# Layer two's gate and value of the last two blocks as one 2x2 block product with seven products

## The chip, the cores and the metric

One core of a Trainium2 chip runs the whole kernel in one launch. The metric is the device time of a run in microseconds, the median over runs; lower is better. The engines are TensorE (PE: matmuls; PEld is its weight load), VectorE (DVE), ScalarE (ACT), GpSimd (POOL) and the DMA queues, of which SyncE (SP) issues all the transfers named here. Each engine works through its own instructions in order and waits for others by semaphores.

## The reference

Attention over 2304 tokens, then two feed-forward layers of width 512. The change is in the second.

```python
attn_out = _attn_ref(**attn_kwargs)            # dense on a mean over 4, plus local
x = ...reshape(B * S, H * D)                   # 2304 x 512
h = x @ w_in                                   # layer one, 512 x 2048
g = np.maximum(h, 0.0) + alpha * np.minimum(h, 0.0)
x = g @ w_out
xn = x / rms * rms_g                           # layer two, 512 x 1536
g = xn @ w_gate
silu = g * (1.0 / (1.0 + np.exp(-g)))
val = xn @ w_val
return silu * val @ w_out
```

## The kernel before

**Numbers.** Every f32 operand of a large product is split into a high and a low f16 half, and a product is made as high x high, high x low and low x high. A product over 512 = KK x 128 inputs so takes 4 x 3 = 12 matmuls. `split` and the pairs "ACT copy to f16, DVE subtraction" make the halves.

**Stages.** The tokens are cut into six blocks (0 to 5) of BW = 384. `m1(m)` is layer one of a block: `h_mm` (L1416, tile hps; ACT relu L1420, DVE L1422), then `o_mm` (L1433, tile acc), copied out by `m1_evac` (L1447) into x1. `rms_tasks(m)` makes the norm of a block: ACT squares (L1349), sums over partitions on PE, a power on POOL (L1375), a broadcast on PE, and per 128 inputs a product (L1390) and a split.

`m2(m, slot)` is layer two of a block, in NF2 = 12 slices f of 128 hidden values. `h_part(f)` makes the gate and the value (`proj`, L1533, tile gps, 12 matmuls of 384 columns each), a tanh on ACT (L1542, th), (th + 1) x gate on DVE (L1544), times value and a scale on DVE (L1547), and the halves uhl: high on ACT (L1553), low on DVE (L1554). `o_part(f)` (L1562) multiplies three groups of 128 tokens by w_out: 9 matmuls of 512 columns into the accumulators oacc0 to oacc2, two slices behind. At the end of a block each accumulator is copied by ACT (L1618) into ob, of which there is one buffer, and stored by SP; so the next copy waits for the store. Block 5 is special: its halves are written in a permuted order (three groups, 32 by 4) so that the output rows lie together, its last two slices run accumulator by accumulator (`o_last`, L1580), and `store_last` (L1586 to L1592) copies each accumulator half on ACT and half on DVE.

**Banks.** The PSUM tags are a0 to a3 (one bank each), w (two) and at (two). The accumulators acc and oacc lie in a0 to a3, gate and value in w, w, a3 in turn.

**Order.** The program is written as a loop over stages (L1755), with side work (attention of later blocks, weight decoding, norms) put between the slices from the queues `urgent` and `bg`, as the tables `feed` and `rms_at` say. `issue_order` then sets the order of every engine by a list scheduler with modelled durations; the table LEADS shifts priorities of ranges of instructions (first, end, by how much), counted in program order. After the first blocks the stages are m2(0), m2(1), m1(2), m1(3), m2(2), m2(3), m1(4), m1(5), m2(4), m2(5).

## Time and profile before

| | us |
|---|---|
| median of 3 runs | 960.71 (960.42 to 963.69) |
| span of the profiled execution | 957.0 |
| TensorE busy in it | 928.3 |
| VectorE busy | 676.8 |
| ScalarE busy | 481.4 |
| GpSimd busy | 128.0 |

The median is 3.7 us longer than the span of the profiled execution. Layer two of block 3 ends near 680 us, m1(4) and m1(5) run to about 805, m2(4) to about 880, m2(5) to the end.

The page gives busy times, slices and groups of instructions; the windows give busy times in a chosen stretch; the chain of waits follows the last instruction back through what released each step; the timeline lists single instructions. A matmul's record lasts until its last value has drained, so the mean duration of a group is longer than the distance from one matmul to the next.

### The profile page before, as it was taken

The page shows a single profiled execution, that of the slowest core. Times are in us where ns is not written, and L with a number is a line of the kernel's source. Part 1 is how long each engine was busy: PE and PEld are TensorE (multiplying, and loading weights), DVE is VectorE, ACT ScalarE, POOL GpSimd, SP SyncE. Part 2 cuts the span into 40 slices and gives each one's busy share as a digit, 9 for nine tenths or more (in the row PEclk, how much of TensorE's full clock was granted, in tenths as well). Part 3 has the DMA queues.
Part 4 walks back from the last instruction along what each step waited for, and adds up shares of the span by engine and source line. Part 5 has one row for each costly group of instructions (what it writes and reads, how often), then busy time and mean ns, then how long its engine had stood idle before and what let it go on. Part 6 is the DMA issues. An engine that isn't in the chain of part 4 may idle for free.

```text
span 957.0 us, 16449 instructions
## 1 busy us (share of the span) xinstructions
PE 928.3 (97%) x6484; PEld 599.6 (63%) x6484; DVE 676.8 (71%) x1333; ACT 481.4 (50%) x1108; POOL 128.0 (13%) x103
## 2 busy tenths in 40 slices
PE   6978999999999999999999999999999999999998
PEld 5667877799555565556666655555566666555554
DVE  4789996899999968999977899973333342442333
ACT  5899989889872472233576322222332433221322
POOL 1101100211022003332102323220000000000000
PEclk9999999999999999999999999999999999999999
DMA  9976444574221241121032120200000000000000
GB/s 214 278 253 177 130 143 130 196 234 137 72 74 58 91 150 50 55 78 55 25 88 84 50 65 20 50 18 1 23 12 1 1 2 1 1 1 12 23 1 34
DMA packets 53711, 73.79 MB, mean 77 GB/s; under 512 B 22190, under 2 KB 35138, under 8 KB 53634
## 3 DMA queue, kind: packets, MB, share of 16 engines
q1 hardware_dynamic: 53634, 72.74, 25.3%
q8 instruction: 51, 0.84, 0.4%
q14 instruction: 26, 0.21, 0.1%
HBM read 68.01 MB, written 4.72 MB: 76 GB/s over the span
## 4 chain that ended last, share of the span: by engine, by line
PE 78%; ACT 4%; DMA 3%; DVE 3%; issue 1%; SPq 0%; ACTq 0%
PE gps L1533 26%; PE acc L1433 16%; PE hps L1416 16%; PE oacc L1562 14%; DMA out_dram<-ob 3%; PE avps L749 1%; PE sps L709 1%; PE atps L737 1%; DMA wr<-in_moe_w_gate_dram 1%; ACT wr L1165 1%; ACT w L415 1%; DVE prod L575 1%; PE xps L612 1%; DVE hps L1422 1%; DVE wc L1167 0%
## 5 line engine op out<-in xcount | busy, mean ns | idle before, releaser
L1416 PE MATMUL hps<-xt,wi 128*128 128x192 f16 (+1 forms) x1536 | 345.9, 289 | 6.6 <-DVE g L416 4.3
L1533 PE MATMUL gps<-x,w 128*128 128x384 f16 x1728 | 349.5, 326 | 0.6 <-ACT x L1447 0.4
L1433 PE MATMUL acc<-ghl,wo 128*128 128x384 f16 (+1 forms) x960 | 249.4, 310 | 0.5 <-ACT ghl L415 0.4
L1533 PEld LDWEIGHTS <-w 128*128 128x128 f16 x1728 | 169.4, 98 | 116.5 <-issue 2.6
L1562 PE MATMUL oacc<-w,uhl 128*128 128x512 f16 x630 | 200.4, 379 | 1.8 <-ACT ob L1618 1.7
L1416 PEld LDWEIGHTS <-wi 128*128 128x128 f16 x1536 | 148.0, 100 | 59.3 <-issue 7.7
L1433 PEld LDWEIGHTS <-wo 128*128 128x128 f16 x1344 | 128.8, 99 | 60.0 <-issue 2.6
L1422 DVE SCALAR_TENSOR_TENSOR hps<-g,oma,hps 128x192 f32<-128x192 f32 (+1 forms) x128 | 66.1, 517 | 66.1 <-ACT g L1420 65.4
L1542 ACT ACTIVATE th<-gps,tsc 128x384 f32<-128x384 f32 x72 | 41.7, 581 | 124.2 <-PE gps L1533 123.9
L1562 PEld LDWEIGHTS <-uhl 128*128 128x128 f16 x630 | 61.8, 98 | 64.3 <-issue 2.5
L1544 DVE SCALAR_TENSOR_TENSOR th<-th,gps 128x384 f32<-128x384 f32 x72 | 39.6, 551 | 84.9 <-ACT th L1542 84.7
L1553 ACT ACTIVATE uhl<-gps 128x384 f16<-128x384 f32 x72 | 41.7, 579 | 107.0 <-DVE gps L1547 98.5
L1420 ACT ACTIVATE g<-hps 128x384 f32<-128x384 f32 x96 | 47.0, 489 | 95.7 <-PE hps L1416 95.4
L521 POOL TENSOR_TENSOR prod<-cq,ckv 128x896 f32<-128x896 f32 x24 | 53.1, 2213 | 172.9 <-DVE ls L532 52.2
L1433 PE MATMUL acc<-g,wo 128*128 128x384 f16 (+1 forms) x384 | 69.8, 286 | 0.0
L1554 DVE TENSOR_TENSOR uhl<-gps,uhl 128x384 f16<-128x384 f32 x72 | 45.4, 630 | 28.4 <-ACT uhl L1553 28.1
L575 POOL TENSOR_TENSOR prod<-ls,ckv 128x896 f32<-128x896 f32 x24 | 47.9, 1997 | 126.4 <-issue 54.8
L416 DVE SCALAR_TENSOR_TENSOR ghl<-hps,grp,ghl 128x384 f16<-128x384 f32 (+1 forms) x73 | 44.3, 608 | 27.0 <-ACT ghl L415 26.7
L415 ACT ACTIVATE ghl<-hps,grp 128x384 f16<-128x384 f32 (+1 forms) x73 | 41.9, 574 | 40.2 <-DVE hps L1422 37.2
L532 DVE TENSOR_REDUCE ls<-prod 128x14 f32<-128x896 f32 x48 | 51.0, 1076 | 0.0
L1162 ACT ACTIVATE wr<-wr 128x768 f32<-128x768 f32 (+1 forms) x48 | 41.5, 874 | 8.7 <-DMA wr<-in_moe_w_val_dram 4.9
L1547 DVE SCALAR_TENSOR_TENSOR gps<-th,kap,gps 128x384 f32<-128x384 f32 x60 | 37.1, 618 | 9.6 <-PE gps L1533 7.0
(240 smaller groups left out, 1143.4 us busy)
## 6 DMA issues: line engine op xcount, KB each, us to landing
wr<-in_moe_w_out_dram SPq DMA_DIRECT2D x18, 512.0 KB
wr<-in_moe_w_in_dram SPq DMA_DIRECT2D x10, 768.0 KB
wr<-in_moe_w_gate_dram SPq DMA_DIRECT2D x8, 768.0 KB
wr<-in_moe_w_val_dram SPq DMA_DIRECT2D x8, 768.0 KB
ckv<-in_k_dram SPq DMA_DIRECT2D x7, 768.0 KB
ckv<-in_v_dram SPq DMA_DIRECT2D x7, 768.0 KB
wr<-in_moe_w_out_dram SPq DMA_DIRECT2D x20, 256.0 KB
sd<-in_q_dram SPq DMA_DIRECT2D x24, 144.0 KB
```

The costliest lines, as they stand in the source:

```text
L415: nc.scalar.activation(out=hi, in_=src, func=AF.Copy, scale=s)
L416: nc.vector.scalar_tensor_tensor(out=lo, in0=src, scalar=s, in1=hi, op0=ALU.mult, op1=ALU.subtract)
L521: engs[i].tensor_tensor(out=pr, in0=view(st["q"][:, j, t:t + TP], [[D, TP], [0, ND], [1, D]]), in1=view(st["k"][:, j, t:t + TP], [[D, TP], ...
L532: nc.vector.tensor_reduce(out=st["s"][:, j, t:t + TP], in_=st.pop(("p", i)), axis=AX.X, op=ALU.add)
L575: engs[i].tensor_tensor(out=over(pr, i), in0=view(st["s"][:, j, t:t + TP], [[ND, TP], [1, ND], [0, D]]), in1=view(st["v"][:, j, t:t + TP], ...
L1416: nc.tensor.matmul(ps[:, j], wi[:, f + j, a, kk * 128:(kk + 1) * 128], x[:, b_, kk, c0:c0 + n], start=(i == 0), stop=(i == 3 * KK - 1))
L1420: nc.scalar.activation(out=g, in_=ps, func=AF.Relu, scale=-1.0)
L1422: nc.vector.scalar_tensor_tensor(out=ps[:, j], in0=g[:, j], scalar=oma[:, f + j:f + j + 1], in1=ps[:, j], op0=ALU.mult, op1=ALU.add)
L1433: nc.tensor.matmul(acc[e], wo_f(f)[:, a, e * 128:(e + 1) * 128], hl[:, b_], start=(f == f0 and i == 0), stop=(f == f1 and i == 2))
L1533: nc.tensor.matmul(ps, w2_t[i0 + f // 3].rearrange("p a (k c) -> p a k c", k=KK)[:, a, kk, (f % 3) * 128:(f % 3 + 1) * 128], xh[:, b_, kk] ...
L1554: nc.vector.tensor_tensor(out=t1, in0=vp, in1=t0, op=ALU.subtract)
L1562: nc.tensor.matmul(acc[tt], t[:, a, tt * 128:(tt + 1) * 128], w[:, b_, f % 3], start=(f in first and i == 0), stop=(f in last and i == 2))
```

## The change

Layer two of blocks 4 and 5 becomes one stage, `m2_pair`. For one slice f the gate and value weights, each cut into two halves of the 512 inputs, form a 2x2 block matrix, and the two blocks of tokens, each cut in the same way, another. Their product is made by Strassen's method (in Winograd's form) with seven block products of 6 matmuls instead of eight. Three of the partial results are copied out of a bank while it still accumulates (`snap`: ACT, L1753, PSUM into SBUF), and three are added to such a copy (`plus`: DVE, L1756). Gates are then read from SBUF (tanh L1760, DVE L1761), and the halves are made by `halves` (ACT L1637, DVE L1638), permuted for block 5 alone. The second products follow for all twelve slices, in the banks a0, at, w, a1, at, a2 and with the copy in two halves; block 4's rows go out by `rows_out`, block 5's as before.

The sums and differences of weights are made by `pair_w` (per three slices 4 additions on POOL, 4 operations on DVE and 4 pairs of halves, all 768 wide), those of the inputs by `pair_x` (4 subtractions on DVE and the halves). They are kept in slices of layer one's weights whose last use is past, and in buffers that are free. In program order three of the four sets of weights are written in m2(3); the scheduler places them all, on POOL, DVE and ACT, among the slices of m1(4) and m1(5), and leaves the differences of the inputs and the norms in m2(3). The norms of blocks 4 and 5 move into layer two of block 3, local attention step 11 into m1(4), and the stages now run m2(2), m1(4), m1(5), m2(3), pair. Some scales change (P_N, P_U, P_G). The table LEADS is the same but for its line breaks, with 63 entries more at its end, whose first are shown.

```diff
-    (2930, 2948, 23500), (2582, 2585, -16500),
...
+    (5918, 6055, 3000), (2930, 2948, 23500), (2582, 2585, -16500), (6303, 6355, -2500), (6304, 6360, -1000),
+    (7303, 7478, 6000), (6691, 6718, -23500), (6590, 6615, -1000), (6906, 7280, 12500), (5813, 5946, 5500),
...
-    P_N, P_U = 10, 44
+    P_N, P_U, P_G = 8, 38, 13
...
+                if m >= PAIR:
+                    y = pair_y(m, e)
+                    nc.vector.scalar_tensor_tensor(out=y, in0=x1_t[m][:, e], scalar=rgx[:, e:e + 1], in1=st["r"],
+                                                   op0=ALU.mult, op1=ALU.mult)
+                    if m == PAIR or e >= KK // 2:
+                        halves(xh_t[m][:, 0, e], xh_t[m][:, 1, e], y)
+                    return
...
-            if m == NBLK - 1:
-                vp = vp.rearrange("p (x t c) -> p x t c", x=NT, c=NC)
-                t0, t1 = [x.rearrange("p (x c t) -> p x t c", x=NT, c=NC) for x in (t0, t1)]
...
-        def o_last():
-            for tt in range(NT):
-                for f in range(NF2 - LA, NF2):
-                    w = w2_t[8 + f // 3].rearrange("p a (f e) -> p a f e", f=3)
-                    for i, (a, b_) in enumerate(((0, 0), (0, 1), (1, 0))):
-                        nc.tensor.matmul(acc[tt], uhl[f][:, a, tt * 128:(tt + 1) * 128], w[:, b_, f % 3],
-                                         start=False, stop=(f == NF2 - 1 and i == 2))
...
+            rows_out(o, m, tt)
+
+    PAIR = NBLK - 2
+    K2 = KK // 2
+    PW = K2 * UC
...
+    def halves(hi, lo, x):
+        nc.scalar.activation(out=hi, in_=x, func=AF.Copy)
+        nc.vector.tensor_tensor(out=lo, in0=x, in1=hi, op=ALU.subtract)
+
+    def pair_y(m, e):
+        o = 6 * 2 * BW + ((m - PAIR) * KK + e) * BW
+        return wo[:, o:o + BW]
...
+        def sub(o, a, b):
+            nc.vector.tensor_tensor(out=o, in0=a, in1=b, op=ALU.subtract)
+
+        def put(n, x):
+            halves(tx[n][:, 0], tx[n][:, 1], x.rearrange("p (k n) -> p k n", k=K2))
+
+        def f1():
+            sub(b11, b12, b11)
+            put(1, b11)
+
+        def f2():
+            sub(b11, b22, b11)
+            put(2, b11)
+
+        def f3():
+            sub(b12, b22, b12)
+            put(3, b12)
+
+        def f4():
+            sub(b21, b21, b11)
+            put(4, b21)
...
+        def full(n):
+            def f():
+                w = w2_t[i + 4 * (n // 2)][:, :, (n % 2) * PW:(n % 2 + 1) * PW]
+                nc.gpsimd.tensor_tensor(out=tmp(n), in0=w[:, 0], in1=w[:, 1], op=ALU.add)
+            return f
+
+        def comb(n, o, a, b, op):
+            def f():
+                nc.vector.tensor_tensor(out=tmp(o), in0=tmp(a), in1=tmp(b), op=op)
+                d = sw[i, n] = pair_dst(i, n)
+                halves(d[:, 0], d[:, 1], tmp(o))
+            return f
+
+        return [full(0), full(2), full(3), full(1), comb(1, 3, 2, 3, ALU.add), comb(3, 2, 0, 2, ALU.subtract),
+                comb(2, 0, 3, 0, ALU.subtract), comb(4, 1, 1, 0, ALU.subtract)]
...
+    def m2_pair():
+        ma, mb = PAIR, PAIR + 1
+        NT = BW // 128
+        scr = [outd_p.tile([128, BW], F32, tag="outd", name="sn") for _ in range(2)]
+        lo = att.tile([128, 2, BW], F32, tag="lo", name="sn")
+        scr += [lo[:, 0], lo[:, 1]]
+        for i in range(4):
+            scr += [w2_t[4 + i][:, a, 0:PW].bitcast(F32) for a in range(2)]
+        last = {}
...
+        def product(ps, w, x, c, start):
+            n = 0
+            for kk in range(K2):
+                for a, b_ in ((0, 0), (0, 1), (1, 0)):
+                    nc.tensor.matmul(ps, w[:, a, kk, c:c + 128], x[:, b_, kk], start=(start and n == 0),
+                                     stop=(n == 3 * K2 - 1), skip_group_check=True)
+                    n += 1
+
+        def snap(o, ps):
+            nc.scalar.activation(out=o, in_=ps, func=AF.Copy)
+
+        def plus(o, ps):
+            nc.vector.tensor_tensor(out=o, in0=ps, in1=o, op=ALU.add)
+
+        def gate(f, g, pool, tag):
+            th = pool.tile([128, BW], F32, tag=tag, name="th")
+            nc.scalar.activation(out=th, in_=g, func=AF.Tanh, scale=tsc[:, f // 3:f // 3 + 1])
+            nc.vector.scalar_tensor_tensor(out=th, in0=th, scalar=1.0, in1=g, op0=ALU.add, op1=ALU.mult)
+            return th
+
+        def value(f, u, v, h):
+            nc.vector.scalar_tensor_tensor(out=u, in0=u, scalar=kap[:, f // 3:f // 3 + 1], in1=v, op0=ALU.mult,
+                                           op1=ALU.mult)
+            t = uhl(f)[:, h]
+            t0, t1 = t[:, 0], t[:, 1]
+            if h:
+                u = u.rearrange("p (x t c) -> p x t c", x=NT, c=NC)
+                t0, t1 = [x.rearrange("p (x c t) -> p x t c", x=NT, c=NC) for x in (t0, t1)]
+            halves(t0, t1, u)
+
+        xa, xb = xh_t[ma], xh_t[mb]
+        b11, b21, b22 = xa[:, :, 0:K2], xa[:, :, K2:KK], xb[:, :, K2:KK]
+        for f in range(NF2):
+            i, c = f // 3, f % 3 * 128
+            s = [sw[i, n].rearrange("p a (k c) -> p a k c", k=K2) for n in range(1, 5)]
+            s1_, s2_, s3_ = [scr[(3 * f + n) % len(scr)] for n in range(3)]
+            ta, tb, tf = f"a{f % 3}", "at", ("w", "w", "a3")[f % 3]
+            A = pool_of(ta).tile([128, BW], F32, tag=ta, name="pa")
+            B_ = pool_of(tb).tile([128, BW], F32, tag=tb, name="pb")
+            F_ = pool_of(tf).tile([128, BW], F32, tag=tf, name="pf")
+            product(A, wv(i, 0), b11, c, True)
+            snap(s1_, A)
+            product(B_, wv(i, K2), b21, c, True)
+            plus(s1_, B_)
+            ga = gate(f, s1_, wk, "mm")
+            product(A, s[1], tx[2], c, False)
+            snap(s2_, A)
+            product(F_, s[0], tx[1], c, True)
+            product(A, s[2], tx[3], c, False)
+            snap(s3_, A)
+            plus(s3_, F_)
+            product(F_, s[3], b22, c, False)
+            plus(s2_, F_)
+            gb = gate(f, s2_, hl_p, "hl")
+            product(A, wv(4 + i, K2), tx[4], c, False)
+            value(f, ga, A, 0)
+            value(f, gb, s3_, 1)
...
+        for h, m in enumerate((ma, mb)):
+            for tt in range(NT):
+                n = h * NT + tt
+                tag = ("a0", "at", "w", "a1", "at", "a2")[n]
+                acc = pool_of(tag).tile([128, DM], F32, tag=tag, name="oacc")
+                for f in range(NF2):
+                    w = w2_t[8 + f // 3].rearrange("p a (f e) -> p a f e", f=3)
+                    for i, (a, b_) in enumerate(((0, 0), (0, 1), (1, 0))):
+                        nc.tensor.matmul(acc, uhl(f)[:, h, a, tt * 128:(tt + 1) * 128], w[:, b_, f % 3],
+                                         start=(f == 0 and i == 0), stop=(f == NF2 - 1 and i == 2))
+                TQ = 128 // NC
+                tag = "prod" if h == 0 else "raw"
                 o = pool_of(tag).tile([128, DM], F32, tag=tag, name="ob")
-                nc.scalar.activation(out=o, in_=acc[tt], func=AF.Copy, scale=col(INV2))
-            TQ = 128 // NC
-            t_abs = m * 2 * T + tt * TQ
-            done = 0
-            while done < TQ:
-                b, t = divmod(t_abs + done, TT)
-                step = min(TQ - done, TT - t)
-                if b == 0 or b == 1 and t < T:
-                    dst = out[b * S + t * NC:b * S + (t + step) * NC, :]
+                HD = DM // 2
+                nc.scalar.activation(out=o[:, 0:HD], in_=acc[:, 0:HD], func=AF.Copy, scale=col(INV2))
+                nc.vector.tensor_scalar(out=o[:, HD:DM], in0=acc[:, HD:DM], scalar1=col(INV2), scalar2=None,
+                                        op0=ALU.mult)
+                if h:
+                    b, t = divmod(m * 2 * T + tt * TQ, TT)
+                    assert t + TQ <= TT and b > 0
+                    nc.sync.dma_start(out=bass.AP(tensor=out.tensor, offset=out.offset + (b * S + t) * DM,
+                                                  ap=[[TT * DM, NC], [DM, TQ], [1, DM]]), in_=o)
                 else:
-                    r0, TL = (CW - T, TT - T) if b == 1 else (0, TT)
-                    dst = bass.AP(tensor=out.tensor, offset=out.offset + (b * S + r0 + t) * DM,
-                                  ap=[[DM, step], [TL * DM, NC], [1, DM]])
-                nc.sync.dma_start(out=dst, in_=o[done * NC:(done + step) * NC])
-                done += step
+                    rows_out(o, m, tt)
...
-        ("m2", 3): local(11),
+        ("m1", 4): local(11),
+        ("m1", 5): pair_w(0),
     }
 
-    rms_at = {"o1": 0, ("m2", 0): 1, ("m1", 3): 2, ("m2", 2): 3, ("m1", 5): 4, ("m2", 4): 5}
+    rms_at = {"o1": 0, ("m2", 0): 1, ("m1", 3): 2, ("m2", 2): 3}
 
     def start(key):
         bg.extend(feed.get(key, []))
+        if key == ("m2", 3):
+            urgent.extend(rms_tasks(PAIR) + rms_tasks(PAIR + 1) + pair_x())
+            for i in (1, 2, 3):
+                bg.extend(pair_w(i))
...
-    for kind, m in (("m2", 0), ("m2", 1), ("m1", 2), ("m1", 3), ("m2", 2), ("m2", 3), ("m1", 4), ("m1", 5), ("m2", 4), ("m2", 5)):
+    for kind, m in (("m2", 0), ("m2", 1), ("m1", 2), ("m1", 3), ("m2", 2), ("m1", 4), ("m1", 5), ("m2", 3)):
...
+    m2_pair()
```

Three places show the new order. First ACT where block 3's (before: block 4's) accumulators are copied out and the next stage starts. Before, ob is the copy of an accumulator, th and uhl are the next block's tanh and high half:

```order
L1542 ACTIVATE th_9706<-gps_9693,tsc_121 128x384
L1553 ACTIVATE uhl_9723<-gps_9709 128x384
L1618 ACTIVATE ob_9753<-oacc0_9208,sc_105 128x512
L1542 ACTIVATE th_9779<-gps_9766,tsc_121 128x384
L1618 ACTIVATE ob_9756<-oacc1_9209,sc_105 128x512
L1553 ACTIVATE uhl_9796<-gps_9782 128x3x4x32
L1542 ACTIVATE th_9812<-gps_9799,tsc_121 128x384
L1553 ACTIVATE uhl_9829<-gps_9815 128x3x4x32
L1618 ACTIVATE ob_9760<-oacc2_9210,sc_105 128x512
L1542 ACTIVATE th_9845<-gps_9832,tsc_121 128x384
```

After, wo and xc hold the halves of the inputs' differences, and sn is the first snapshots' tile:

```order
L1637 ACTIVATE xc_8712<-wo_108 128x768
L1629 ACTIVATE ob_9309<-oacc0_8675,sc_105 128x512
L1637 ACTIVATE xc_8712<-wo_108 128x768
L1753 ACTIVATE sn_9318<-pa_9321 128x384
L1753 ACTIVATE sn_9319<-pa_9321 128x384
L1629 ACTIVATE ob_9312<-oacc1_8676,sc_105 128x512
L1760 ACTIVATE th_9338<-sn_9318,tsc_121 128x384
L1753 ACTIVATE sn_9320<-pa_9321 128x384
L1753 ACTIVATE sn_9320<-pa_9384 128x384
L1753 ACTIVATE w2_2779<-pa_9384 128x384
L1629 ACTIVATE ob_9315<-oacc2_8677,sc_105 128x512
L1760 ACTIVATE th_9401<-sn_9320,tsc_121 128x384
```

The copies ob stand among the snapshots (sn, w2), the tanhs and the last halves of the inputs, instead of among one tanh and one high half per slice.

Second, ACT inside the stage. Before, block 5 alternates:

```order
L1542 ACTIVATE th_9845<-gps_9832,tsc_121 128x384
L1553 ACTIVATE uhl_9862<-gps_9848 128x3x4x32
L1542 ACTIVATE th_9887<-gps_9874,tsc_121 128x384
L1553 ACTIVATE uhl_9904<-gps_9890 128x3x4x32
L1542 ACTIVATE th_9929<-gps_9916,tsc_121 128x384
L1553 ACTIVATE uhl_9946<-gps_9932 128x3x4x32
L1542 ACTIVATE th_9971<-gps_9958,tsc_121 128x384
```

After, in the pair (pa is the bank with the chain, sn and w2 the places of snapshots; wo holds the high halves, 128x3x4x32 the permuted ones):

```order
L1753 ACTIVATE sn_9318<-pa_9573 128x384
L1760 ACTIVATE th_9527<-w2_3685,tsc_121 128x384
L1760 ACTIVATE th_9558<-w2_4015,tsc_121 128x384
L1753 ACTIVATE sn_9319<-pa_9573 128x384
L1637 ACTIVATE wo_108<-th_9558 128x3x4x32
L1753 ACTIVATE sn_9320<-pa_9636 128x384
L1753 ACTIVATE sn_9320<-pa_9573 128x384
L1637 ACTIVATE wo_108<-th_9527 128x384
L1760 ACTIVATE th_9590<-sn_9318,tsc_121 128x384
L1753 ACTIVATE w2_2779<-pa_9636 128x384 x2
L1753 ACTIVATE w2_3320<-pa_9699 128x384
L1760 ACTIVATE th_9621<-sn_9319,tsc_121 128x384
```

Between two snapshots of one slice there now stand up to two tanhs or high halves of other slices.

Third, the start of SP's queue: loads of q, k and v (wo, sdv), of small rows, and of layer one's weights (wr). Before:

```order
L795 DMA wo_108<-in_k_dram 96x6x64
L795 DMA wo_108<-in_q_dram 96x6x64
L1143 DMA wr_663<-in_moe_w_in_dram 128x2x768
L795 DMA wo_108<-in_q_dram 96x6x64
L795 DMA wo_108<-in_k_dram 96x6x64
L803 DMA sdv_160<-in_v_dram 72x2x512
L1695 DMA rows_176<-in_moe_alpha_dram 16x128
L1695 DMA rows_176<-in_moe2_rms_g_dram 4x128
L1143 DMA wr_665<-in_moe_w_in_dram 128x2x768
```

After:

```order
L813 DMA wo_108<-in_k_dram 96x6x64
L813 DMA wo_108<-in_q_dram 96x6x64 x2
L813 DMA wo_108<-in_k_dram 96x6x64
L821 DMA sdv_160<-in_v_dram 72x2x512
L1888 DMA rows_176<-in_moe_alpha_dram 16x128
L1161 DMA wr_663<-in_moe_w_in_dram 128x2x768
L1888 DMA rows_176<-in_moe2_rms_g_dram 4x128
L813 DMA wo_108<-in_q_dram 96x6x64
L821 DMA sdv_166<-in_v_dram 72x2x512
```

The first load of layer one's weights now stands behind a load of q, k, v and the small rows that it used to precede, and the second (wr_665) further back.

## Rows read from the trace of the kernel before

**Rows 1.** Busy table of the page; then PE in 40 slices, in tenths

```profile
PE 928.3 (97%) x6484; PEld 599.6 (63%) x6484; DVE 676.8 (71%) x1333; ACT 481.4 (50%) x1108; POOL 128.0 (13%) x103
...
PE   6978999999999999999999999999999999999998
```

**Rows 2.** Windows: stretch, length, busy us of each engine, granted clock, DMA share, GB/s

```profile
0.00:128.00 128.00, 109.29 (x1003) 87.81 (x1003) 102.56 (x282) 110.19 (x320) 15.37 (x43) 0.97 0.74 209
...
240.00:260.00 20.00, 17.95 (x128) 11.79 (x128) 18.82 (x34) 16.69 (x26) 1.84 (x1) 1.00 0.19 63
...
678.00:805.00 127.00, 127.00 (x783) 76.98 (x782) 47.77 (x85) 43.67 (x86) 0.85 (x1) 1.00 0.03 7
805.00:880.00 75.00, 75.00 (x434) 42.66 (x433) 27.47 (x50) 20.31 (x42) 0.85 (x1) 1.00 0.00 1
880.00:900.00 20.00, 18.12 (x107) 10.29 (x106) 6.41 (x9) 6.09 (x9) 0.00 (x0) 1.00 0.14 39
900.00:950.00 50.00, 50.00 (x281) 27.24 (x279) 19.51 (x27) 14.11 (x18) 0.00 (x0) 1.00 0.00 1
950.00:957.00 7.00, 2.60 (x12) 0.89 (x10) 1.66 (x4) 1.42 (x3) 0.00 (x0) 0.88 0.30 112
```

**Rows 3.** Chain of waits, late part: start us, us, engine, line, instructions

```profile
809.97 5.85 PE gps L1533 x36
...
874.78 3.90 PE oacc L1562 x18
878.71 0.70 ACT ob L1618
879.42 5.84 DMA out_dram<-ob
885.34 0.70 ACT ob L1618
886.65 7.50 DMA out_dram<-ob
894.25 0.70 ACT ob L1618
894.99 0.81 PE oacc L1562 x3
```

**Rows 4.** Groups of instructions: gate and value matmuls

```profile
L1533 PE MATMUL gps<-x,w 128*128 128x384 f16 x1728 | 349.5, 326 | 0.6 <-ACT x L1447 0.4
```

**Rows 5.** Timeline of ACT after block 3: start, us, instruction, idle before

```profile
680.02 0.69 ACT L1618 ACTIVATE ob<-oacc,sc 128x512 f32<-128x512 f32 x1 [1.76 <-PE oacc L1562]
...
686.66 0.69 ACT L1618 ACTIVATE ob<-oacc,sc 128x512 f32<-128x512 f32 x1 [1.61 <-DMA out_dram<-ob]
...
693.27 0.69 ACT L1618 ACTIVATE ob<-oacc,sc 128x512 f32<-128x512 f32 x1 [1.22 <-DMA out_dram<-ob]
```

**Rows 6.** Groups by form, whole span: operations that the pair repeats

```profile
L1420 ACT ACTIVATE g<-hps 128x384 f32<-128x384 f32 x96 | 47.0, 489 | 95.7 <-PE hps L1416 95.4
...
L1542 ACT ACTIVATE th<-gps,tsc 128x384 f32<-128x384 f32 x72 | 41.7, 581 | 124.2 <-PE gps L1533 123.9
...
L1544 DVE SCALAR_TENSOR_TENSOR th<-th,gps 128x384 f32<-128x384 f32 x72 | 39.6, 551 | 84.9 <-ACT th L1542 84.7
...
L1547 DVE SCALAR_TENSOR_TENSOR gps<-th,kap,gps 128x384 f32<-128x384 f32 x60 | 37.1, 618 | 9.6 <-PE gps L1533 7.0
...
L1390 DVE TENSOR_TENSOR ra<-x,rps 128x384 f32<-128x384 f32 x24 | 12.7, 548 | 3.8 <-PE rps L1381 3.6
```

**Rows 7.** Groups by form, 900 to 957 us: the permuted halves of block 5

```profile
L1553 ACT ACTIVATE uhl<-gps 128x384 f16<-128x384 f32 x9 | 9.2, 1027 | 12.7 <-DVE gps L1547 12.7
L1554 DVE TENSOR_TENSOR uhl<-gps,uhl 128x384 f16<-128x384 f32 x9 | 9.1, 1015 | 10.4 <-ACT uhl L1553 10.4
```

**Rows 8.** Waits of PE, 0 to 130 us: total us, times, longest

```profile
PE hps L1416 <- DVE g L416: 4.3, 4, 2.5
PE tps L844 <- DMA wo<-in_q_dram: 4.1, 2, 3.0
```

More of the change, by code (lines that the diff above doesn't have):

```diff
@@ L1301, in f @@
             e, sc_ = eb2[:, i:i + 1], sw2[:, i:i + 1]
-            pow2(y, e, sc_, P_W, over_parts(y))
+            pow2(y, e, sc_, P_G if i < 8 else P_W, over_parts(y))
             if i < 4:
                 nc.vector.tensor_scalar(out=tsc[:, i:i + 1], in0=e, scalar1=rg2[:, 1:2],
-                                        scalar2=0.5 * 2.0 ** -(P_N + P_W), op0=ALU.mult, op1=ALU.mult)
+                                        scalar2=0.5 * 2.0 ** -(P_N + P_G), op0=ALU.mult, op1=ALU.mult)
             elif i >= 8:
@@ L1518, in m1_first, with rows_out @@
                         acc = m1_acc(n)
+    def rows_out(o, m, tt):
+        TQ = 128 // NC
+        t_abs = m * 2 * T + tt * TQ
+        done = 0
+        while done < TQ:
+            b, t = divmod(t_abs + done, TT)
+            step = min(TQ - done, TT - t)
+            if b == 0 or b == 1 and t < T:
+                dst = out[b * S + t * NC:b * S + (t + step) * NC, :]
+            else:
+                r0, TL = (CW - T, TT - T) if b == 1 else (0, TT)
+                dst = bass.AP(tensor=out.tensor, offset=out.offset + (b * S + r0 + t) * DM,
+                              ap=[[DM, step], [TL * DM, NC], [1, DM]])
+            nc.sync.dma_start(out=dst, in_=o[done * NC:(done + step) * NC])
+            done += step
     def m2(m, slot):
@@ L1602, in m2 @@
                 h_part(f)
-            if f >= LA and not (ends and f >= NF2):
+            if f >= LA:
                 o_part(f - LA)
@@ L1606, in m2 @@
                 slot(f, NF2)
-        if ends:
-            o_last()
         for tt in range(NT):
@@ new lines, with pair_dst @@
+    sw = {}
+    stmp = {}
+    def pair_dst(i, n):
+        u = 4 * i + n - 1
+        if u < 4:
+            if ("r", u // 2) not in sw:
+                sw["r", u // 2] = raw_p.tile([128, 2 * PW], F32, tag="raw", name="wsr")
+            return sw["r", u // 2][:, u % 2 * PW:(u % 2 + 1) * PW].bitcast(F16).rearrange("p (a w) -> p a w", a=2)
+        if u < 14:
+            o = (u - 4) * 2 * PW
+            return wi.rearrange("p f a c -> p (f a c)")[:, o:o + 2 * PW].rearrange("p (a w) -> p a w", a=2)
+        if u == 14:
+            sw["x"] = x1_p.tile([128, 2 * PW], F32, tag="x1", name="wsx")
+        return sw["x"][:, (u - 14) * PW:(u - 13) * PW].bitcast(F16).rearrange("p (a w) -> p a w", a=2)
@@ new lines, in pair_w, with tmp @@
+    def pair_w(i):
+        st = {}
+        def tmp(n):
+            if not stmp:
+                r = raw_p.tile([128, 2 * PW], F32, tag="raw", name="wt")
+                stmp[0], stmp[1] = r[:, 0:PW], r[:, PW:2 * PW]
+                for j in (2, 3):
+                    stmp[j] = prod_p.tile([128, PW], F32, tag="prod", name="wt")
+            return stmp[n]
+        def full(n):
[11 more added lines that the diff above has]
+                comb(2, 0, 3, 0, ALU.subtract), comb(4, 1, 1, 0, ALU.subtract)]
```

39 lines of the change are left out of this document (22 added, 17 removed), and 71 rows, old and new, of the table LEADS.

## Prediction

> **What bounds the kernel now.** I read the busy table first: TensorE (PE) is busy 97% of the span, VectorE (DVE) 71%, ScalarE (ACT) 50% [rows 1]. A matmul that goes is therefore worth nearly its full time, as long as PE does not begin to wait where it goes. The slices show where PE has gaps: almost only in the first tenth [rows 1]. The windows put numbers on that [rows 2]: of 28.7 us of idle PE (957.0 - 928.3), 18.7 lie in the first 128 us, 2.05 in 240 to 260, 1.88 in 880 to 900, 4.4 in the last 7. From 678 to 880 and from 900 to 950, layer two's last stretches among them, PE has no gap at all, at a granted clock of 1.00, the 2.4 GHz level, while DVE is busy 38 to 39% and ACT 28 to 34%. The change acts in that last part, so its price list is PE's.
>
> What a matmul costs there is not its row in the table of groups: a record of 326 ns [rows 4] includes a drain that lies beside the next one. The chain of waits gives the step: 36 matmuls of 384 columns in 5.85 us, 162.5 ns each, and 18 of 512 columns in 3.90 us, 216 ns each [rows 3]. The drain, 326 - 162.5, says instead when a result may be read: some 0.2 us after the last matmul's slot.
>
> The Trainium skill ("TensorE: Matmul & The Clock Gate", section "Back-to-back issue gap") says that in a long stream of weight load and matmul the spacing is about 81 ns at 128 columns and 131 ns at 512, and that the width divided by 2.4 plus 2.5 holds for a lone matmul only. Between its two figures 384 columns would take an estimated 114 ns, and the 72 removed matmuls would be worth 8.2 us. The rows above, taken in just such a stream, are 162.5 and 216, which is the formula that it keeps for the lone one; I go by the rows.
>
> **The products.** Gate and value of blocks 4 and 5 took 12 slices f, each 24 matmuls in each of two blocks: 576. With seven products of 6 matmuls it is 42 per f, 504 in all. The other four blocks keep theirs, and the second products (oacc) stay 216 in number. So 72 matmuls of 384 columns go: 72 x 0.1625 = **-11.7 us**, all of it in a stretch without idle time.
>
> **The bubble between blocks 4 and 5.** PE waits there because there is one output buffer: an accumulator can be copied out only when the store of the one before has landed. The chain shows it [rows 3]: copy 0.70, transfer 5.84, copy 0.70, transfer 7.50, copy 0.70, and only then oacc. With both blocks in one stage this hand-over is gone: **-1.9 us** (all idle of 880 to 900). Another takes its place, block 3 to the pair. There the copies are 6.64 us apart as at 680.02, 686.66 and 693.27 [rows 5]. In the new order the first product needs bank a0, free after the first copy; f=1 needs a1, free 6.64 + 0.69 after that copy began, and PE gets to it some 7.1 us after it, by the number of matmuls between; so it is late by about **+0.3 us**. Bank a2, for f=2, is reached another 6.8 us on, about when it comes free. On ACT the second and third copies wait in line for a store, with snapshots and tanhs behind them; I leave this in the upper bound of the next term.
>
> **What the pair needs from ACT and DVE.** Each f now has a chain through one bank: product, snapshot into SBUF, product on top, snapshot, product, snapshot, product, value. A snapshot is a copy of 384 columns from PSUM: 489 ns, as L1420 [rows 6]. Per f ACT has 3 of these, two tanhs of 581, a plain copy (priced as L1420 too) and a permuted one of 1.03 [rows 6, 7]: 4.15 us. DVE has 3 sums of 548 (as L1390, SBUF with PSUM), two of 551, two of 618, a plain remainder (priced as L1390 too) and a permuted one of 1.01 [rows 6, 7]: 5.5 us. PE has 42 x 0.1625 = 6.83 us. So PE remains the bound by load, with ACT at 61% and DVE at 80%, double what they had there [rows 2].
>
> By latency it is closer. Between two products on one bank PE's order has 5 to 7 matmuls of other products, 0.81 to 1.14 us; a snapshot needs 0.2 + 0.49 + 0.05 = 0.74. That fits if ACT is free. If a tanh stands ahead of it, it is 1.3, with the permuted copy 1.8, and PE waits up to 0.5 to 0.9 us. ACT's order puts tanhs and copies between the snapshots in every f, as the change section shows. The second chain has 10 to 15 matmuls, 1.6 to 2.4 us, for a snapshot and a sum of 1.3, and rarely waits. I walked f=4 and f=5 through all five orders with the durations above: PE waited 0.58 us in the two together, about 0.25 per f, **+3 us** in 12. Bounds: 0, if each snapshot comes just in time; +6.6, if in every f one snapshot stands behind one tanh (0.55 each).
>
> **What hides the preparation.** Sums of weights (16 on GpSimd, 16 on DVE, each then halved by ACT and DVE) stand in layer one of blocks 4 and 5, the differences of the inputs and the norms of blocks 4 and 5 in layer two of block 3. For a 768-wide sum on DVE twice L1547's 618 ns is enough: 32 x 1.24 = 40 us, beside 16 on ACT (16 x 2 x 0.49). The cover is a stretch of some 200 us in which DVE is at 38% and ACT at a third of PE's time [rows 2], and GpSimd does nearly nothing (0.85 of 127): cost **0**. Without that cover it would show as idle PE in front of the first product. Halving the differences has least room: it stands ahead of the first copy of block 3's output on ACT.
>
> **The early order.** The table of leads shifts also loads, weight decodes and matmuls of the first 130 us and around 200 to 260 us; from about the tenth gate of layer one the two orders agree again. PE waits there 4.3 us for DVE's gates and 4.1 for a load [rows 8], both among what moved. No row prices a reordering: **0**, between -2 (the gap of 240 to 260 gone) and +3 (a load late by the longest that one kept PE waiting, 3.0).
>
> **End.** The last two accumulators still end one after the other, with the same halves and the same fast stores: 0.
>
> **Rivals.**
> (a) The orders fit better than my walk: no waits in the pair, early part up to 2 us better: -11.7 - 1.9 + 0.3 - 0 to 2 = -13.3 to -15.3, 945.4 to 947.4. For it: ACT and DVE have spare time. Against: tanhs stand before snapshots in each f. I allow 944 to 948.
> (b) The chain costs 0.6 to 1 us per f, since a delay on ACT moves every later snapshot too: 7 to 12 us for 3, so 954.4 to 959.4. For it: DVE at 80% with two ops behind each tanh. Against: waits don't add up where PE runs 6.8 us for ACT's 4.15.
> (c) The early order loses 3 us or more: 953 to 958.
> (d) Slower: each of the four turnarounds per f (after three snapshots, and on the other bank) comes late behind a tanh, a permuted copy or a waiting output copy, so that the pair runs at ACT's and DVE's latency. From 0.31 us each, 48 x 0.31 = 15 us, it eats all of 13.6 and more: 962 at 0.31, and at 0.5 (one tanh each) 24 us, 971. It decides from 13 us of waits. Against: it takes a busy ACT at each turnaround, and ACT is free 39% of the time.
> (e) The change does not do what it says, since 72 matmuls fewer are all paid in waits at the hand-over and in the pair: 958 to 962. The middle between (b) and (d).
>
> **The numbers.** Sum: -11.7 - 1.9 + 0.3 + 3 + 0 + 0 = -10.3. Against the profiled execution that is 957.0 - 10.3 = 946.7 of span. The median of the runs, 960.71, is 3.7 over that span, which stays: **950.4 us**. Chances: the forecast (948 to 953.5) 0.56, (a) 0.15, (b) 0.16, (c) 0.05, (d) 0.04, (e) 0.04. Range: from (a)'s better half, 945.5, to (b)'s upper part, 958; some 0.15 is left out, mostly above. A difference under 0.5% can't be told from none here; that is 955.9 to 965.5. Faster by more: all of the forecast and (a), half of (b), half of (c): 0.82. Within: the rest of (b) and (c), (e) and a part of (d): 0.14. Slower by over 0.5%: 0.04.
>
> **What would show it.** In the profile after: PE matmuls of 384 columns 72 fewer, with a step still 162.5 ns; a PE busy time in the pair and its oacc of about 82 + 47 us; PE idle in the pair with ACT's snapshot as its releaser, about 3 us (over 7: (b); over 13: (d); under 1: (a)); no gap between blocks 4 and 5, and one of about 0.3 us at f=1 behind the output copy; PE idle before 128 us near 18.7 and in the 20 us around 250 near 2 (else (c)). The prediction fails if ACT turns out to wait on DVE for each halved value before it can take the next snapshot, if the differences of the inputs are late, or if a step of a matmul that adds onto a bank is longer than 162.5 ns.

## The result and the profile after

The changed kernel takes 948.88 us (median of 4 runs, 948.27 to 950.21) for 960.57 before; the ratio of the runs on record is 0.9889 (95% interval 0.9863 to 0.9916), which is 10.7 us off (8.1 to 13.2); the two medians by themselves lie 11.7 apart. In a second comparison it is 949.39, ratio 0.9888 (0.9866 to 0.9910). Forecast were 950.4, that is 10.3 off. The two profiled executions stand at 957.0 and 948.5 us of span, 8.5 apart; why that is less is told below.

The busy table and the slices of the page after, which answer to [rows 1]:

```profile
PE 917.4 (97%) x6412; PEld 593.4 (63%) x6412; DVE 726.9 (77%) x1410; ACT 508.3 (54%) x1162; POOL 152.8 (16%) x119
...
PE   7977999999999999999999999999999999999997
```

72 matmuls fewer (6412 for 6484), 10.9 us less of PE, 50 us more of DVE, 27 more of ACT, and PE is still the engine at 97%. The windows after, with the columns of [rows 2]; layer two of block 3 ends near 811, the pair's products near 896:

```profile
0.00:128.00 128.00, 107.90 (x991) 87.31 (x992) 100.48 (x277) 108.15 (x316) 14.70 (x43) 0.92 0.73 207
...
540.00:610.00 70.00, 69.51 (x408) 40.10 (x407) 65.68 (x109) 20.27 (x42) 21.29 (x13) 1.00 0.15 40
610.00:700.00 90.00, 89.24 (x547) 53.82 (x546) 72.48 (x110) 38.15 (x74) 27.21 (x16) 1.00 0.04 10
700.00:800.00 100.00, 100.00 (x603) 59.23 (x602) 48.90 (x79) 32.76 (x63) 8.27 (x6) 1.00 0.00 1
...
812.00:830.00 18.00, 17.80 (x108) 10.37 (x107) 10.64 (x19) 8.52 (x15) 0.00 (x0) 1.00 0.17 44
830.00:850.00 20.00, 19.62 (x120) 11.48 (x118) 15.32 (x27) 12.18 (x22) 0.00 (x0) 1.00 0.00 1
...
870.00:895.00 25.00, 24.63 (x152) 14.59 (x151) 18.53 (x33) 14.87 (x25) 0.00 (x0) 1.00 0.00 1
895.00:940.00 45.00, 45.00 (x213) 20.74 (x212) 8.10 (x15) 5.22 (x10) 0.00 (x0) 1.00 0.09 24
940.00:948.50 8.50, 3.71 (x18) 1.47 (x15) 0.97 (x2) 0.95 (x2) 0.00 (x0) 0.86 0.17 62
```

In the pair PE idles 0.15 to 0.4 us in each 18 to 25 us, DVE is at 74 to 77% and ACT at 59 to 61% once all is running: the load that was worked out, 80 and 61%. The 20 us with the 1.88 us bubble of [rows 2] have no counterpart. The waits of PE from 540 to 700 us, where the kernel before has none (total, times, longest):

```profile
PE acc L1458 <- ACT ob L1629: 0.8, 2, 0.5
PE oacc L1600 <- ACT uhl L1591: 0.5, 1, 0.5
```

The first stands where layer one of block 4 now follows layer two of block 2. The second belongs to the early order and not to the stages: the kernel before with the new early entries (below) has the same wait of 0.5 us there. These are the waits of PE from 780 us on:

```profile
PE pa L1748 <- ACT w L1753: 0.7, 4, 0.2
```

### The profile page after: what moved, and what is told of

Same layout as the page of the kernel before. It is cut to its first block, busy times and chain, and to the rows that moved or that the text cites. A ratio compares the mean times of both kernels' runs of the same rounds, so it can differ in the third digit from the quotient of the medians.

```text
span 948.5 us, 16472 instructions
## 1 busy us (share of the span) xinstructions
PE 917.4 (97%) x6412; PEld 593.4 (63%) x6412; DVE 726.9 (77%) x1410; ACT 508.3 (54%) x1162; POOL 152.8 (16%) x119
## 4 chain that ended last, share of the span: by engine, by line
PE 76%; DVE 7%; DMA 7%; ACT 6%; issue 2%; SPq 1%; ACTq 0%; DVEq 0%
PE gps L1574 17%; PE hps L1441 16%; PE acc L1458 15%; PE oacc L1600 9%; PE oacc L1810 5%; PE pa L1748 3%; DMA out_dram<-ob 2%; PE pf L1748 2%; DMA wr<-in_moe_w_gate_dram 2%; ACT wr L1180 1%; DVE prod L593 1%; PE lsps L950 1%; SPq L813 1%; ACT wr L1183 1%; PE sps L727 1%
## 5 line engine op out<-in xcount | busy, mean ns | idle before, releaser
L1458 PE MATMUL acc<-ghl,wo 128*128 128x384 f16 (+1 forms) x960 | 245.9, 310 | 1.9 <-DVE ghl L434 0.9
L1574 PE MATMUL gps<-x,w 128*128 128x384 f16 x1152 | 244.7, 326 | 0.7 <-DVE uhl L1592 0.7
L1574 PEld LDWEIGHTS <-w 128*128 128x128 f16 x1152 | 112.8, 99 | 77.4 <-issue 3.2
L1600 PE MATMUL oacc<-w,uhl 128*128 128x512 f16 x432 | 144.8, 379 | 0.5 <-ACT uhl L1591 0.5
L1600 PEld LDWEIGHTS <-uhl 128*128 128x128 f16 x432 | 42.8, 99 | 41.5 <-ACT uhl L1591 0.9
L1583 ACT ACTIVATE th<-gps,tsc 128x384 f32<-128x384 f32 x48 | 27.6, 580 | 62.7 <-PE gps L1574 62.5
L1591 ACT ACTIVATE uhl<-gps 128x384 f16<-128x384 f32 x48 | 23.3, 488 | 69.3 <-DVE gps L1588 50.4
L1810 PE MATMUL oacc<-w,wo 128*128 128x512 f16 x180 | 42.3, 380 | 0.0
L1585 DVE SCALAR_TENSOR_TENSOR th<-th,gps 128x384 f32<-128x384 f32 x48 | 26.3, 551 | 19.4 <-ACT th L1583 18.7
L1183 ACT ACTIVATE wr<-wr,nhalf 128x768 int32<-128x768 uint32 (+1 forms) x40 | 39.5, 988 | 0.0
```

The costliest lines, as they stand in the source:

```text
L1183: nc.scalar.activation(out=lo, in_=lo.bitcast(mybir.dt.uint32), func=AF.Relu, scale=2.0 ** -29, bias=nhalf)
L1458: nc.tensor.matmul(acc[e], wo_f(f)[:, a, e * 128:(e + 1) * 128], hl[:, b_], start=(f == f0 and i == 0), stop=(f == f1 and i == 2))
L1574: nc.tensor.matmul(ps, w2_t[i0 + f // 3].rearrange("p a (k c) -> p a k c", k=KK)[:, a, kk, (f % 3) * 128:(f % 3 + 1) * 128], xh[:, b_, kk] ...
L1600: nc.tensor.matmul(acc[tt], t[:, a, tt * 128:(tt + 1) * 128], w[:, b_, f % 3], start=(f in first and i == 0), stop=(f in last and i == 2))
L1810: nc.tensor.matmul(acc, uhl(f)[:, h, a, tt * 128:(tt + 1) * 128], w[:, b_, f % 3], start=(f == 0 and i == 0), stop=(f == NF2 - 1 and i == 2))
```

## What was asked of the chip

The theory: PE bounds the pair, so a matmul there is worth its step, and the chains of snapshots cost a few us of waits. The rivals: the chains set the pace, or the early order made the difference. The measure for the pair is the stretch from the first copy of block 3's output to the start of the last copy of all. In the changed kernel (timeline of ACT):

```profile
810.28 0.69 ACT L1629 ACTIVATE ob<-oacc,sc 128x512 f32<-128x512 f32 x1 [0.46 <-PE oacc L1600]
...
943.75 0.47 ACT L1816 ACTIVATE ob<-oacc,sc 128x256 f32<-128x256 f32 x1 [0.39 <-PE oacc L1810]
```

133.47 us, and 133.47 again in a second execution (811.05 to 944.52) and in the run with the old early order (812.88 to 946.35). What happens ahead of it drops out. Two things have to be the same before two stretches are compared, or be counted: how many matmuls of block 3's oacc still fall into it (11 here), and how PE's lost time is read. PE's timeline (824 to 830 us) shows the second:

```profile
826.25 0.33 PE L1748 MATMUL pf<-xc,wsr 128*128 128x384 f16 x1
826.79 0.32 PE L1748 MATMUL pa<-xc,w 128*128 128x384 f16 x1 [0.20 <-ACT w L1753]
```

The two starts are 0.54 us apart, 0.37 more than a step of 0.1625, but the gap reads 0.20, because the first record goes on after its step. By starts, nine matmuls of the stretch come late, by 2.4 us together; seven of them show a gap, and the gaps add up to 1.1. Below, "lost by starts" is that first sum.

### An eighth product, and a scheduler that moved everything

```diff
             product(F_, s[0], tx[1], c, True)
+            product(F_, s[0], tx[1], c, True)
```

> The changed kernel with one product more: the first product into the second chain's bank is made twice per slice (the second making overwrites the first), so that there are 8 products of 6 matmuls again, 72 matmuls of 384 columns more, and the chain of snapshots stays. Theory (TensorE bounds the pair, a matmul is worth its step): 72 x 0.1625 = 11.7 us more than the changed kernel's 948.9, less the 1 us of waits that the added work can cover: 959.6 to 960.6. Rival (the gain comes from the merged stage and its order, and the pair waits for something else): 949 to 954.

Measured: 994.88 us, ratio 1.0357 (1.0320 to 1.0393): 46 us more, outside every case. The stretch tells that the pair is not the place:

```profile
847.97 0.69 ACT L1629 ACTIVATE ob<-oacc,sc 128x512 f32<-128x512 f32 x1 [0.46 <-PE oacc L1600]
...
991.26 0.47 ACT L1817 ACTIVATE ob<-oacc,sc 128x256 f32<-128x256 f32 x1 [0.39 <-PE oacc L1811]
```

143.29 us, 9.8 more; the other 37.7 us were lost ahead of it (847.97 for 810.28). The scheduler weighs every instruction by what still follows it and keeps the best of many rounds; six matmuls per slice at the end gave another base order for the whole program, to which the table of leads, fitted to instruction numbers, no longer belongs. So the run was made again with the added matmuls counted as taking no time. That leaves every engine's order as it was up to 660 us, and from there to the pair but for some exchanges on PE and DVE:

```diff
+            PIN.update({x.name: 0.0 for x in nc.cur_bb.bb.instructions[n0:]})
...
-    dur = [cost(k, *aps[k]) for k in count]
+    dur = [PIN.get(insts[k].name, cost(k, *aps[k])) for k in count]
```

> The changed kernel with the first product of the second chain made twice again (72 matmuls of 384 columns more), but with the scheduler told that they take no time, so that every engine's order up to the pair is that of the changed kernel; in the first run with eight products the scheduler had chosen another order for the whole program, and 37 us were lost ahead of the pair. Theory (a matmul in the pair is worth its step, the added ones cover up to 2 us of waits): 949.4 + 11.7 - 0 to 2 = 959.1 to 961.1, the pair's stretch from the first copy of block 3's output to the last copy 143 to 145 for 133.5. Rival (the pair's pace is set by its chains): 949 to 954.

Measured: 959.32 us, ratio to before 0.9989 (0.9977 to 1.0001). The stretch:

```profile
808.91 0.69 ACT L1632 ACTIVATE ob<-oacc,sc 128x512 f32<-128x512 f32 x1 [0.55 <-PE oacc L1603]
...
952.14 0.47 ACT L1822 ACTIVATE ob<-oacc,sc 128x256 f32<-128x256 f32 x1 [0.39 <-PE oacc L1816]
```

143.23 us: 9.76 more in the stretch, 9.9 in the median. The added matmuls are 72 x 0.1625 = 11.7, and they cover 1.9 us of waits: lost by starts are 0.4 us for 2.4. So 143.23 - 11.7 - 0.4 = 131.1 would be the stretch with seven products and no waits at all, and the waits of the pair cost 133.47 - 131.1 = 2.4 us. The rival (the chains set the pace) falls for seven products.

### One product less

```diff
-            product(F_, s[3], b22, c, False)
```

> The changed kernel without the last product of the second chain in each slice, six products for seven (that part of the sum is left out). Theory (TensorE bounds the pair, and ACT and DVE have slack): TensorE needs 5.85 us per slice, DVE 5.5; 11.7 us less, and up to 4 us of new waits since each turnaround has fewer matmuls to hide behind: 937 to 941.5. Rival (the pair already runs near the latency of its snapshots and sums): less than half of the 11.7 comes, 943 to 949.

Measured: 949.92 us, ratio 0.9887 (0.9858 to 0.9915): no gain at all, less than even the rival allowed. The stretch says otherwise:

```profile
822.44 0.67 ACT L1629 ACTIVATE ob<-oacc,sc 128x512 f32<-128x512 f32 x1
...
944.25 0.47 ACT L1815 ACTIVATE ob<-oacc,sc 128x256 f32<-128x256 f32 x1 [0.39 <-PE oacc L1809]
```

121.81 us, 11.66 less. That is not quite like for like: 6 of block 3's matmuls fall into it for 11, and the five missing ones are worth 5 x 0.216 = 1.1. For equal work it is 10.6 less, the 11.7 of the 72 matmuls but for 0.9 us of new waits (3.3 lost by starts). The scheduler had again chosen another order, here from 538 us on, and 12.2 us went ahead of the stretch. With the orders kept (the last product cut from 384 columns to 8, the scheduler told that it takes as long as before):

```diff
-            product(F_, s[3], b22, c, False)
+            product(F_[:, 0:8], s[3], b22[:, :, :, 0:8], c, False)
```

> The changed kernel with the last product of the second chain cut from 384 to 8 columns (that part of the sum is left out), all orders unchanged. Theory (TensorE still sets the pace with a sixth less to do, as the stretch of the first run with six products says, 121.8 for 133.5): 72 matmuls cost 60 to 100 ns each for 162.5, 4.5 to 7.4 us less and up to 2 us of waits back: 942 to 947. Rival (chains set the pace): 948 to 949.5.

Measured: 946.74 us, ratio 0.9856 (0.9838 to 0.9873); the stretch is 130.67 (809.83 to 940.50), 2.8 less. PE's waits from 795 us on:

```profile
PE pa L1751 <- ACT w L1756: 4.5, 10, 1.0
PE pa L1751 <- ACT sn L1756: 1.1, 2, 0.8
PE pa L1751 <- ACT ob L1632: 0.4, 1, 0.4
```

The short matmuls freed more than was expected: the next matmul starts 26 ns after one of 8 columns, not 60 to 100, so 72 x (162.5 - 26) = 9.8 us were there to gain. But waits for snapshots grow from 0.7 to 5.6 us, and the time lost by starts from 2.4 to 9.2: in this order the chain's turnarounds lose the matmuls that covered them, and most of the gain goes. Both runs together: the loads of ACT and DVE leave room for six products, but not in the order made for seven. The order for seven is near the edge.

### The merged stage with plain products

```diff
+            ga = gate(f, whole(0, xa, ta), wk, "mm")
+            value(f, ga, whole(4, xa, "w"), 0)
+            gb = gate(f, whole(0, xb, tf), hl_p, "hl")
+            value(f, gb, whole(4, xb, "at"), 1)
```

(`whole` makes 12 matmuls over all 512 inputs; products, snapshots and sums are gone, and block 5's first 256 inputs are halved too.)

> The changed kernel with blocks 4 and 5 still in one stage, but gate and value made as plain products over all 512 inputs, 8 x 6 matmuls per slice, without snapshots and sums; the preparation of weights and inputs is still done, for nothing. Theory: the stage merge alone is worth the bubble of 1.9 us less what the hand-over costs, so 960.6 - 1.9 + 0 to 1.5 of early order = 958.7 to 960.5, and within 1.5 us of the run with eight products and the chain. Rival (the chain of snapshots costs several us, hidden in the total): 4 us or more below the run with eight products, at 955 to 957.

Measured: 958.50 us (10 runs, 957.12 to 961.22), just below the theory's 958.7, ratio 0.9984 (0.9970 to 0.9999). Merging the stages alone is worth 1.5 us (0.1 to 2.9), which holds the bubble of 1.9 less what the new order of blocks costs. The stretch:

```profile
808.82 0.69 ACT L1629 ACTIVATE ob<-oacc,sc 128x512 f32<-128x512 f32 x1 [0.77 <-PE oacc L1600]
...
950.76 0.47 ACT L1810 ACTIVATE ob<-oacc,sc 128x256 f32<-128x256 f32 x1 [0.39 <-PE oacc L1804]
```

141.94 us, with 7 of block 3's matmuls for 11, so 142.8 for equal work, and nothing is lost by starts. With eight products and the chain it was 143.23, of which 0.4 is lost: with that much other work the chain is nearly free. The step from the plain stage to the changed kernel, 142.8 - 133.47 = 9.3 us, is the saved product less the waits: 11.7 - 2.4. The medians say 958.5 - 949.4 = 9.1.

### What the pair waits for

```diff
         def snap(o, ps):
             nc.scalar.activation(out=o, in_=ps, func=AF.Copy)
+            nc.scalar.activation(out=o, in_=ps, func=AF.Copy)
```

> The changed kernel with every snapshot made twice on ACT: 36 x 0.49 = 17.6 us more of ACT, 5.6 of 6.8 us per slice, and each link of the first chain 1.23 us for 0.74, against 0.81 to 1.14 of other matmuls. Theory (a little slack on each link): three links per slice late by 0.1 to 0.4 us, 12 x 3 x 0.15 = 5 us, range 2 to 10: 951 to 959. Rival 1 (no slack, the whole addition is paid): 948.9 + 17.6 = 966 or more. Rival 2 (TensorE runs far ahead of the snapshots, all hidden): 949.

Measured: 952.44 us (5 runs, 949.77 to 955.22), ratio 0.9914 (0.9887 to 0.9942). The stretch is 134.33 (809.00 to 943.33), 0.9 more, and 1.3 more for equal work (9 of block 3's matmuls for 11); lost by starts are 3.7 us for 2.4. The waits from 780 us on:

```profile
PE pa L1748 <- ACT w L1754: 0.8, 2, 0.5
PE pf L1748 <- DVE sn L1757: 0.7, 2, 0.4
PE pa L1748 <- ACT sn L1754: 0.5, 1, 0.5
```

17.6 us more of ACT cost 1.3 us of stretch, below the theory's 2 to 10 and nearly rival 2, all hidden. The median is 3 us up, within the theory's 951 to 959; the stretch, read in the fastest of the five executions, doesn't show the rest. Up to 755 us the order is that of the changed kernel, and the spread of the start (below) is wide enough for it, but no run shows that it is the cause. So a snapshot's length is a small part of what the pair waits for. The run without the permutation shows the large one:

```diff
-            if h:
+            if False:
                 u = u.rearrange("p (x t c) -> p x t c", x=NT, c=NC)
```

> The changed kernel with block 5's halves written in plain order (its output rows come out permuted, the work is the same): the high half on ACT falls from 1.03 to 0.49 us, the low one on DVE from 1.01 to 0.55, 12 of each. Theory (of 1.1 us of waits in the pair most stand behind a permuted copy, nothing else hangs on it): 948 to 948.5, the waits of the pair below 0.6. Rival (the copies set the pair's pace): 12 x 1 = 12 us off, below 940.

Measured: 947.38 us, ratio 0.9864 (0.9843 to 0.9885). All orders are those of the changed kernel. The stretch:

```profile
807.91 0.69 ACT L1629 ACTIVATE ob<-oacc,sc 128x512 f32<-128x512 f32 x1 [0.46 <-PE oacc L1600]
...
939.49 0.47 ACT L1816 ACTIVATE ob<-oacc,sc 128x256 f32<-128x256 f32 x1 [0.39 <-PE oacc L1810]
```

131.58 us, 1.9 less, more than the 1.1 of gaps that had been expected to go at most. Lost by starts are 0.5 us for 2.4, and those 0.5 stand at the hand-over, up to 825 us. The chain of the changed kernel shows the path. Between 830 and 896 us it leaves PE for more than a single step at four places, and three of them read like this one (start, us, engine, line):

```profile
860.59 0.49 ACT w L1753
861.08 0.96 ACT wo L1637
862.06 1.02 DVE wo L1638
863.09 0.39 DVE w L1756
863.50 0.62 ACT th L1760
864.12 0.38 ACT w L1753
864.55 0.32 PE pa L1748
```

A permuted high half on ACT, its low half on DVE, and behind that on DVE the sum (L1756) of another slice, which is late by a microsecond. Here a tanh waits for that sum, and behind the tanh, on ACT, the snapshot that PE is waiting for; at the other two (832.34 and 887.01) PE's second chain waits for the sum itself. PE's wait names the snapshot, since that stood last in line; at the head of the line is the permuted pair.

### A version that permutes once

```diff
+                    if m > PAIR:
+                        yo = y.rearrange("p (x c t) -> p x t c", x=NT, c=NC)
...
+                        nc.vector.tensor_tensor(out=yo, in0=xi, in1=r, op=ALU.mult)
+                        nc.scalar.activation(out=y, in_=y, func=AF.Copy, scale=rgx[:, e:e + 1])
...
-            if h:
-                u = u.rearrange("p (x t c) -> p x t c", x=NT, c=NC)
```

> The changed kernel with block 5's tokens permuted once, where its normalised inputs are written (4 permuted products on DVE and 4 scalings on ACT in layer two of block 3), so that the 24 permuted halves in the pair become plain ones; the result is the same. Theory (the pair's 1.9 us of lost time stand behind the permuted halves, as the run without a permutation shows): the stretch from the first copy of block 3's output to the last one 131.6 for 133.5, total 947.0 to 948.0. Rival (the four permuted products come late at the hand-over and cost as much): 949 to 950.

Measured: 947.64 us (946.86 to 948.17), ratio 0.9864 (0.9849 to 0.9878). The stretch:

```profile
808.06 0.69 ACT L1635 ACTIVATE ob<-oacc,sc 128x512 f32<-128x512 f32 x1 [0.67 <-PE oacc L1606]
...
940.40 0.47 ACT L1819 ACTIVATE ob<-oacc,sc 128x256 f32<-128x256 f32 x1 [0.39 <-PE oacc L1813]
```

132.34 us, 1.1 less than the changed kernel, where 131.6 had been expected. The pair itself waits no more after 823 us; 0.9 us of waits for snapshots (1.2 lost by starts) stand in the first 15, at the hand-over. It is the fastest version here that leaves nothing out. By the totals its interval still touches that of the changed kernel; by the stretch it is ahead.

### The early order

LEADS has 65 new entries, not 63. The 51 of them that end ahead of layer one of block 4 (the last ends at instruction 6101) are taken out of the changed kernel, or put into the one before; 14 stay. The first lines of the first edit:

```diff
-    (7303, 7478, 6000), (6691, 6718, -23500), (6590, 6615, -1000), (6906, 7280, 12500), (5813, 5946, 5500),
-    (3809, 3815, -37500), (6465, 6522, 3500), (2835, 2888, 4000), (5928, 5997, 1500), (5775, 5784, 6000),
...
+    (7303, 7478, 6000), (6691, 6718, -23500), (6590, 6615, -1000), (6906, 7280, 12500), (6465, 6522, 3500),
...
```

> The changed kernel without the 51 new entries of the table of leads that shift instructions ahead of layer one of block 4 (the 14 later ones stay), so that everything up to layer two of block 2 is ordered as before the change. Theory (the new early order costs about 1.5 to 2 us, which the two profiles show as a first copy of block 1's output at 401.4 for 399.8 and of block 2's at 612.9 for 610.8): 947 to 947.5. Rival (the early lateness is the execution's own, a lower granted clock between 40 and 80 us): 948.9 and block 2's copy at the same time as in the changed kernel, within 1 us from run to run.

> The kernel before with those 51 entries added and nothing else. Theory (the new early order costs 1.5 to 2 us): 962 to 962.5. Rival (it costs nothing): 960.6. Third (it gains, and the change's profile was a slow one): 958 to 959.

> The changed kernel once more, as the partner of the two runs on the early order: 948.9, with the clock between 40 and 80 us and the time of block 2's first copy (612.9 in the first profile) as they fall in another execution. If the early lateness is the execution's own, that time moves by over 1 us; if it is the order's, it stays.

Measured, in one comparison of 5 rounds: without the new early entries 951.52 us, ratio 0.9894 (0.9868 to 0.9921); the changed kernel as it is 949.39, 0.9888 (0.9866 to 0.9910); the kernel before with the new entries 959.84, 1.0001 (0.9984 to 1.0019). The theory that the new order costs 1.5 to 2 us falls: on the kernel before it costs 0.1 us (1.5 less to 1.8 more). Nor does the changed kernel gain from the old one: the two ratios are alike.

What the test by block 2's first copy says is less sharp. Between the two executions of the changed kernel it moves by 0.8 us (612.86 and 613.64), less than the 1 us that had been set as the sign of the execution's own spread. Over the eight executions with its order up to there it lies between 610.46 and 613.64, and with the old early order it comes at 615.49. Block 1's first copy decides, since the kernel before and the changed one with the old early order run the same order up to 560 us: it starts at 399.81 in the one and 403.28 in the other, 3.5 us apart. Most of that lateness is therefore the execution's own. A smaller part is not: from block 1's first copy to block 2's the kernel before takes 210.95 us and 211.53 with the new entries; those eight take 211.5 to 211.7, and the changed kernel with the old entries 212.21.

The granted clock is not the execution's own. Over a whole execution its mean is 0.994 to 0.998 in all 54 with the old early order (48 of the kernel before, 6 of the changed one) and 0.985 to 0.995 in all 62 with the new one. By the totals the new order gains elsewhere what it pays in clock.

## Why the prediction was right

**The products**, -11.7: right. 72 matmuls fewer, records still 326 ns [rows 4], and the eighth product put back costs 9.8 with 1.9 of waits covered. The step of 512 columns in a dense stream is as it was, 216 ns, by the chain's row of the second products:

```profile
897.74 45.99 PE oacc L1810 x213
```

**The bubble**, -1.9 and +0.3: the bubble is gone, and the hand-over to the pair is small (the copies start at 810.28, 816.91 and 823.50, 6.6 apart as in [rows 5], and 0.5 us is lost by starts there). What was overlooked is the other new neighbour. Layer one of block 4 now follows layer two of block 2, and its four accumulators need the banks whose copies wait for the stores: 0.8 us. The working had followed the moved blocks only to the pair, not to the place that they left.

**The waits of the pair**, +3 within 0 to 6.6: 2.4 together with the hand-over, for 3.3 forecast. The term held in size, its mechanism not, and that the size came out is in part luck. The step that failed is the rule that a snapshot behind a tanh or a copy on ACT is late in every slice: doubling the snapshots costs only 1.3 us, so ACT's own queue has reserve. Without permuted halves 1.9 of the 2.4 is gone. By the chain it is the low one of them, on DVE, that holds up the sums, which the working had called "rarely" late; no run took the high and the low half away separately.

**Preparation**, 0: right. The sums of weights run on POOL and DVE from 614 to about 730 us (two halves of the last set follow on ACT at 806). PE's only wait between 610 and 700 us is the 0.8 for the banks, and from 700 to 800 it is busy for 100.00 us, with DVE at 49%.

**The early order**, 0 within -2 to +3: right, 0.1 (-1.5 to +1.8).

**The end**, 0: 4.8 us of idle PE after 940 us for 4.4 [rows 2], +0.4. The last stores take longer to end after the last matmul; why was not looked into.

Sum by what the runs showed: -11.7 - 1.9 + 0.8 + 2.4 + 0.4 + 0 = -10.0, where -10.3 was forecast and 10.7 measured (8.1 to 13.2).

**The frame of the sum** was wrong in one point. The 3.7 us between the span of before and its median were taken to lie around the span. In the runs with a listed span that is 1.7 to 1.8 us (2.0 to 2.1 in the four with six products); the other 2 are that the profiled execution of before was shorter than the median one. Since the sum was taken off the median too, the forecast did not suffer, but the difference of the two spans, 8.5, is not the effect: it compares an execution 2 us below the median with one above it (950.21, the longest of the four).

Two readings of the rows are a little off and change nothing: in the stretches without gaps DVE is busy 37 to 39% and ACT 27 to 34% [rows 2], not 38 to 39 and 28 to 34.

Of the rivals, (b), (d) and (e) needed 7 us of waits and more; they are out at seven products. (c) falls with the early order, which costs nothing. Of (a) the total of 948.88 comes near its 948, but not its reason: the pair does wait, and the early order gains nothing. The run with six products in the kept order is the place where (b)'s mechanism shows, with 6.0 us of waits.

## What to carry to other kernels

A product saved on the engine that bounds is worth its step for as long as the chains beside it keep enough other matmuls between their links; measure that reserve by taking one product more away, not by the loads. Look for the wait behind the wait: the releaser named is the last in its line, and the long instruction ahead of it can often be moved to where it runs once (here 24 permuted halves into 4 permuted inputs). Where a scheduler orders the whole program by its total length, an experiment at the end changes the beginning; keep the order fixed, or compare a stretch and not the total.
